# One PSUM tile for the four output banks, tiles visited two at a time, first products in sub-steps: a chunk attention with two FFNs on one core

## The chip, the cores and the metric

One core of one Trainium2 chip runs the kernel. The metric is the device time of one execution in microseconds; before the change it is 1147.26 us, the median of three runs from 1143.62 to 1149.77.

## The reference, cut to what matters

```python
for c in range(S // 32):                               # q, k, v: (4, 8, 768, 64)
    k_full = concat([mem_k, k[16 left, 32 own, 8 right]])   # the same for v
    a = softmax(q_c @ k_full.T / 8)
    out[c] = a @ v_full
x = out.transpose(0, 2, 1, 3).reshape(3072, 512)
g = s * max(x @ w_in, 0) ** 2 + b                      # first FFN, 512 -> 2048 -> 512
x = g @ w_out
h = x @ w_in2                                          # second FFN, same widths
y = (max(h, 0) + alpha * min(h, 0)) @ w_out2
```

## The kernel before

**Tiles and blocks.** The 3072 tokens are 24 attention tiles of 128 tokens, and four tiles make one of six blocks of 512. Each FFN walks over the blocks, and in a block over 16 slices f of the hidden width. One unit is one block with one f: a *first product* (`g1`, L597-608, 12 matmuls of 128x512 into a bank `ph`), the activation on ACT and DVE (L616-650), and a *second product* (`g2`, L651-666, three matmuls for each of four output parts d, into banks `po0` to `po3`, which add up over all f). The factor three is there because every fp32 number is split into a high and a low part in a shorter type, and high·high, high·low and low·high are summed. The weights come as 32-bit words from HBM and are split on chip by `convert` (L286-340) on DVE and ACT.

**Ends of a block.** After the last f of a block the four banks `po` are emptied: in the first FFN ACT writes the high part (L696), then DVE the low part (L700), and GpSimd's DMA queue stores both (`x1_out`, L703); in the second FFN d0 and d2 are copied by ACT (L712), d1 and d3 by DVE (L714), each into one of two buffers (`ao`), and stored. In the last block each copy is split into a half on ACT (L709) and a half on DVE (L710). Blocks 0 and 1 of the first FFN are run in two parts, the first SEG slices of both, and then the rest: at the end of a first part ACT copies the banks out (L676) and they are stored; at the end of the second part DVE adds them back (L688), and high and low are made from the sum. The next block's second products start in bank `po0` right after one more first product (12 matmuls), then follow d1, d2, d3.

**Attention.** A tile has scores (64 matmuls, L401), row maxima, exponentials, sums and normalisation on DVE and ACT, four transposes (*turns*, L466), values (64 matmuls, L488), and a high and a low part of the result on ACT and DVE (L507-514). Tiles 0 to 3 run alone at the start, in the `po` banks, which are free then: `ALONE` maps a tile to a pair of banks, and scores and values lie in two tiles of one bank each, so that DVE and ACT read each bank by an operation of its own (256 columns wide). For a later tile the matmuls are done in a *visit* in one double bank `pa`: scores of tile i and values of tile i-1 in a single step (`products`, L492), and then the turns of tile i by themselves (`turn_joint`, L500).

**Order.** Every step is planned with a duration, a rank, and the steps that it needs (classes `Plan`, `Pace`, `Step`, L70-220); the planner lists the steps by rank and by a model of when each can begin, and the program is emitted in that order (L903-908). The tables `FIRST_LOADS`, `TILE_RANKS`, `BY_HEAD`, `CONV_RANKS` and `STEPS` at the top steer it. The semaphore waits are put in when the program is built: an instruction waits for the last earlier user of a tile that it overwrites or reads. A tile is what one call of `psum.tile` returns.

Of the kernel before, what the change touches and what calls it, by code (L numbers as in the profile page):

```python
# [16 lines left out]
P = 128  # L17
# [10 lines left out]
BLK = 512  # L28
# [17 lines left out]
FIRST_LOADS = """q0 q1 w1i v0 q3 w0o q2 v2 w0i v1 w1o q4 v3 w2 w3 w4 v4 w6 q5 v7 q6 v5 q7 w5 w9 v6 w7 w8""".split()  # L46

TILE_RANKS = (-280, -85, -170, -175, -15, -240, -5, -260, -85)

BY_HEAD = (1, 2, 4, 5, 6)  # L50

CONV_RANKS = {1: 195, 2: 35, 3: 30, 4: 25, 5: 20, 6: 15, 9: -40, 10: -95, 11: -25, 12: -10, 13: 40, 14: -70}

STEPS = (28, 18, 18, 47, 43, 38)
# [28 lines left out]
class Pace:  # L83
# [3 lines left out]
    BLOCK, FIRST = 256, 184  # L87
# [14 lines left out]
    def run(self, t, step, fetch):  # L102

        done, total = 0, max(step.count, 1)
        while done < total:
            at = self.count + done
            block, into = divmod(at - self.FIRST, self.BLOCK)
            if block >= 0 and into == 0:
                t = max(t, self.due[block])
                self.due[block + 1] = t + fetch(t)  # L110
            n = min(total - done, self.BLOCK - into)
# [14 lines left out]
class Plan:  # L126
# [4 lines left out]
    RATE = 396e3  # L131
    LANES = 8
    FETCH = 2.7, 5.3
# [13 lines left out]
    def order(self):  # L147
# [17 lines left out]
        while len(done) < len(self.steps):  # L165
# [58 lines left out]
def tile_chunk_attention_two_ffn(ctx: ExitStack, tc: tile.TileContext, qt, kw, vw, win, wout, cst, out):  # L224
# [11 lines left out]
    xl = [const.tile([P, KD, BLK], F32R, name=f"xl{n}") for n in range(2)]  # L236
    x1d = [dram.tile([P, KD, 2, BLK], F32R, name=f"x1d{j}") for j in range(NB)]
# [27 lines left out]
    wts, raws, conv_done, load_done = {}, {}, {}, {}  # L265

# [19 lines left out]
    def convert(layer, f, mats, rank, after):  # L286
# [106 lines left out]
    def scores(i, banks=None):  # L393
        kd, qT = sets[set_of(i)][0], state[i]["q"]
        banks = banks or bank_pair(i, "sc")
        parts, both = banks if isinstance(banks, tuple) else (banks, None)
        for hp in range(HP):
            for c in range(NC4):
                for par in range(2):
                    r = slice(par * D, par * D + D)  # L400
                    nc.tensor.matmul(parts[par][c * CH:(c + 1) * CH, 0, hp, :],  # L401
                                     lhsT=qT[r, hp, c * CH:(c + 1) * CH], rhs=kd[r, hp, c * (CH + NM):c * (CH + NM) + NKEY],
                                     start=True, stop=True)
        state[i]["sc"] = pieces(parts, both, 0)

    def pieces(parts, both, which):

        if both is not None:
            return [(slice(0, 2), both[:, :, which])]
        return [(slice(par, par + 1), parts[par][:, which:which + 1]) for par in range(2)]  # L410
# [49 lines left out]
    def one_bank(i, name):  # L460
        return psum.tile([P, HP, P], F32, tag=f"po{2 * ALONE[i]}", name=name)
# [15 lines left out]
    def values(i, banks=None):  # L477
# [3 lines left out]
        parts, both = banks if isinstance(banks, tuple) else (banks, None)  # L481
        for half in range(HP // 2):
            for c in range(NC4):
                for odd in range(2):
                    for par in range(2):
                        r, hp = slice(par * D, par * D + D), 2 * half + odd
                        out = parts[par][odd * D:odd * D + D, 1].rearrange("p a n -> p (a n)")
                        nc.tensor.matmul(out[:, half * P + c * CH:half * P + (c + 1) * CH], lhsT=vd[r, c, hp, :],  # L488
                                         rhs=aT[r, hp, c * CH:(c + 1) * CH], start=True, stop=True)
        state[i]["px"] = [(pars, px.rearrange("p two (half a) n -> p two half (a n)", half=HP // 2)) for pars, px in pieces(parts, both, 1)]  # L490

    def products(prev, i):  # L492
# [26 lines left out]
    def softmax(i, r, sc):  # L519
        a = att[i]  # L520
        mx = plan.add("DVE", (0.8 if i % TB in (0, TB - 1) else 0.61) + (0.08 if i in ALONE else 0), r + STEPS[0], lambda: maxima(i), [sc])
# [6 lines left out]
        else:  # L528
            sh = plan.add("DVE", 0.61 + (0.08 if i in ALONE else 0), r + STEPS[0], lambda: shifted(i), [mx])
# [5 lines left out]
    def loads(i, r):  # L535
# [5 lines left out]
        a["lv"] = plan.add("SP", 0.45, first_load(f"v{i}") if early else r - 14, lambda: load_v(i), [left.get("v")], nbytes=1 << 19)  # L541
# [3 lines left out]
    def finish_tile(i, r, px):  # L545
        leaves[set_of(i)]["v"] = leaves[set_of(i)]["x"] = px
        more = 0.15 if i in ALONE else 0
# [433 lines left out]
```

## Time and profile before

| | |
|---|---|
| median of the runs | 1147.26 us |
| the profiled execution, its own time | 1147.76 us |
| its span in the trace | 1146.0 us |
| before and behind the span | 1.76 us |
| instructions in the span | 18300 |
| matmuls that the page lists on PE | 7848 |
| DMA traffic | 98.32 MB |

The span runs from the first to the last instruction of the trace. PE, DVE, ACT, POOL and SP are the five engines (TensorE, VectorE, ScalarE, GpSimd, SyncE), and PEld is the loading of weights into TensorE, which overlaps its matmuls. In a timeline a row gives the start, the duration, the engine, the source line, the operation and its tiles, and in brackets how long the engine was idle just before and what released it. The duration of a matmul covers its pipeline too, so that two that follow each other overlap; what a stream costs is read from the distance between starts.

### The profile page before, as it was taken

What the parts mean: (1) busy time and instruction counts of PE and PEld (TensorE: products, weight loads), DVE (VectorE), ACT (ScalarE), POOL (GpSimd) and SP (SyncE); (2) the same over time, 40 slices, a digit from 0 to 9 for tenths busy, and PEclk for the clock granted to TensorE, in tenths of its full rate; (3) what the DMA queues carried; (4) which work ended last, traced back from release to release, by engine and by line L of the source; (5) the groups of instructions that cost most, each with busy time, mean ns of one, the idle gap of its engine ahead of it and who ended that gap; (6) DMA issues with size and microseconds to landing.
All of it is one profiled execution on the core that took longest, in us unless ns stands there. A gap on an engine that the chain in (4) does not pass through costs nothing.

```text
span 1146.0 us, 18300 instructions
## 1 busy us (share of the span) xinstructions
PE 1117.8 (98%) x7848; PEld 926.0 (81%) x7848; DVE 607.9 (53%) x942; ACT 350.9 (31%) x615; POOL 28.8 (3%) x58
## 2 busy tenths in 40 slices
PE   4799999999999999999999999999999999999998
PEld 4788888888888888888887788888888888888886
DVE  6796945454544445434799844434433434344333
ACT  5675734332223223224565311111111111111111
POOL 0000000000000000000000000000000000000000
PEclk9899999999999999999999999999999999999999
DMA  9918013423113113004557102002002002000000
GB/s 345 351 38 302 10 66 110 146 82 125 51 42 138 42 42 134 1 1 170 198 184 255 76 1 101 10 1 94 17 1 92 19 1 89 23 1 4 34 1 37
DMA packets 46241, 98.32 MB, mean 86 GB/s; under 512 B 4944, under 2 KB 4944, under 8 KB 46160
## 3 DMA queue, kind: packets, MB, share of 16 engines
q1 hardware_dynamic: 40320, 77.22, 19.4%
q0 software_dynamic: 5696, 19.93, 4.6%
q8 instruction: 61, 1.00, 0.4%
q14 instruction: 20, 0.16, 0.0%
q10 hardware_dynamic: 144, 0.01, 0.0%
HBM read 76.16 MB, written 20.97 MB: 85 GB/s over the span
## 4 chain that ended last, share of the span: by engine, by line
PE 49%; issue 42%; DMA 3%; DVE 3%; POOL 1%; ACT 1%; SPq 0%; POOLq 0%; DVEq 0%; ACTq 0%
PE ph L605 24%; PE po L666 22%; PE po L664 2%; DMA raw<-in_win_dram 1%; POOL x1d L703 1%; DVE a L309 1%; DMA spill<-os 1%; DVE a L314 1%; DMA qT<-in_qt_dram 0%; PE sp L488 0%; DMA qa<-in_qt_dram 0%; DMA vd<-in_vw_dram 0%; DVE w L327 0%; DVE gl L649 0%; DMA x1d<-o 0%
## 5 line engine op out<-in xcount | busy, mean ns | idle before, releaser
L605 PE MATMUL ph<-xh,w 128*128 128x512 f32 (+1 forms) x1560 | 509.7, 389 | 1.6 <-issue 0.9
L605 PEld LDWEIGHTS ph<-xh,w 128*128 128x128 f32 x1560 | 293.7, 189 | 61.7 <-DVE g L636 1.1
L605 PE MATMUL ph<-xl,w 128*128 128x512 f32 (+1 forms) x780 | 302.0, 387 | 0.0
L644 ACT ACTIVATE gh<-g 128x512 fp32r<-128x512 f32 (+1 forms) x195 | 121.7, 624 | 465.8 <-DVE g L636 385.2
L664 PE MATMUL po<-gh,w 128*128 128x512 f32 (+1 forms) x792 | 257.9, 387 | 0.2 <-DVE o L688 0.2
L666 PE MATMUL po<-w,gh 128*128 128x512 f32 x768 | 251.6, 389 | 0.5 <-DVE o L700 0.5
L649 DVE TENSOR_TENSOR gl<-g,gh 128x512 fp32r<-128x512 f32 (+1 forms) x195 | 133.1, 683 | 101.7 <-ACT gh L644 100.2
L631 DVE TENSOR_SCALAR g<-ph,cst_sb 128x512 f32<-128x512 f32 x96 | 72.0, 750 | 213.2 <-PE ph L605 213.1
L664 PEld LDWEIGHTS po<-gh,w 128*128 128x128 f32 x792 | 148.7, 189 | 30.1 <-DVE o L688 0.7
L605 PEld LDWEIGHTS ph<-xl,w 128*128 128x128 f32 x780 | 147.6, 189 | 28.6
L666 PEld LDWEIGHTS po<-w,gh 128*128 128x128 f32 x768 | 144.1, 188 | 31.0 <-DVE o L700 1.2
L664 PE MATMUL po<-gl,w 128*128 128x512 f32 (+1 forms) x396 | 152.1, 384 | 0.0
L666 PE MATMUL po<-w,gl 128*128 128x512 f32 x384 | 149.4, 389 | 0.0
L616 ACT ACTIVATE g<-ph 128x512 f32<-128x512 f32 (+1 forms) x99 | 57.8, 584 | 137.7 <-PE ph L605 134.2
L664 PEld LDWEIGHTS po<-gl,w 128*128 128x128 f32 x396 | 75.0, 189 | 14.1
L623 DVE TENSOR_TENSOR g<-g 128x512 f32<-128x512 f32 x48 | 33.2, 692 | 97.0 <-ACT g L616 96.9
L666 PEld LDWEIGHTS po<-w,gl 128*128 128x128 f32 x384 | 72.1, 188 | 14.9
L627 DVE TENSOR_SCALAR g<-g,cst_sb 128x512 f32<-128x512 f32 (+1 forms) x99 | 52.6, 531 | 42.6 <-ACT g L621 41.3
L636 DVE SCALAR_TENSOR_TENSOR g<-ph,g 128x512 f32<-128x512 f32 x96 | 66.3, 690 | 2.9
L296 ACT ACTIVATE a<-raw 128x1024 f32<-128x1024 f32 (+1 forms) x36 | 37.6, 1045 | 22.6 <-DVE w L327 14.3
L321 ACT ACTIVATE w<-a 128x1024 fp32r<-128x1024 f32 (+1 forms) x36 | 34.8, 967 | 31.2 <-DVE a L314 30.1
L327 DVE TENSOR_TENSOR w<-a,w 128x1024 fp32r<-128x1024 f32 (+1 forms) x36 | 39.5, 1100 | 1.2 <-ACT w L321 1.2
(83 smaller groups left out, 517.6 us busy)
## 6 DMA issues: line engine op xcount, KB each, us to landing
raw<-in_win_dram SPq DMA_DIRECT2D x64, 256.0 KB, 4.7
raw<-in_wout_dram SPq DMA_DIRECT2D x64, 256.0 KB, 5.3
x1d<-o POOLq DMA_DIRECT2D x24, 512.0 KB, 3.4
vd<-in_vw_dram SPq DMA_DIRECT2D x40, 256.0 KB, 4.1
kd<-in_kw_dram SPq DMA_DIRECT2D x20, 368.0 KB, 5.0
xh<-x1d SPq DMA_DIRECT2D x6, 1024.0 KB, 5.6
xl<-x1d SPq DMA_DIRECT2D x6, 1024.0 KB, 7.6
qT<-in_qt_dram SPq DMA_DIRECT2D x20, 256.0 KB, 3.9
```

The source lines that it names most:

```text
L296: nc.scalar.activation(out=temp["a"], in_=words(1).bitcast(F32), func=ACTF.Abs)
L321: nc.scalar.activation(out=w[:, :, 0, :], in_=temp["a"], func=ACTF.Copy)
L327: nc.vector.tensor_sub(out=w[:, :, 1, :], in0=temp["a"], in1=w[:, :, 0, :].bitcast(F32))
L605: nc.tensor.matmul(p, lhsT=w[:, a, kk * P:(kk + 1) * P], rhs=x[:, kk, cols], start=(i == 0), stop=(i == 3 * KD - 1))
L616: nc.scalar.activation(out=new_g(u), in_=ph.pop(u), func=ACTF.Relu)
L627: nc.vector.tensor_scalar(out=g, in0=g, scalar1=cst_sb[:, 0:1], scalar2=cst_sb[:, 1:2], op0=ALU.mult, op1=ALU.add)
L631: nc.vector.tensor_scalar(out=new_g(u), in0=ph[u], scalar1=0.0, scalar2=cst_sb[:, 2 + f:3 + f], op0=ALU.min, op1=ALU.mult)
L636: nc.vector.scalar_tensor_tensor(out=g, in0=ph.pop(u), scalar=0.0, in1=g, op0=ALU.max, op1=ALU.add)
L644: nc.scalar.activation(out=gh, in_=gt[u], func=ACTF.Copy)
L649: nc.vector.tensor_sub(out=gl, in0=gt.pop(u), in1=gh.bitcast(F32))
L664: nc.tensor.matmul(po[d][:, cols], lhsT=w[:, a, ds_], rhs=g, start=start, stop=stop)
L666: nc.tensor.matmul(po[d], lhsT=g[:, ds_], rhs=w[:, a, :], start=start, stop=stop)
```

## The change

1. **One tile for the four output banks.** `po_all` is one PSUM tile of four banks, and `po[d]` a slice of it; the four tiles `po0` to `po3` are gone. Tiles 0 to 3 take two-bank slices of it too, and DVE and ACT read both banks by one operation 512 columns wide instead of two of 256.
2. **Tiles 8 to 23 two at a time** (`attention_of_two`): scores of two tiles in one visit, turns of two in the next, values of two in the third.
3. **First products in sub-steps**, for blocks 0 and 1 of the first FFN and f < 6: high·high first, then the four matmuls with the weight's low part and the four with x's low part, each a step of its own that needs only its own operands.
4. **The last block's copies** are no longer halved; all four are on ACT.
5. **The order:** SEG goes from 7 to 8, and the tables and some constants of the planner's model are new.

```diff
-SEG = 7
+SEG = 8
+APART = 6
...
+    po_all = psum.tile([P, KD, BLK], F32, name="po")
+    po = [po_all[:, d] for d in range(KD)]
...
         if i in ALONE:
-            return [psum.tile([P, 2, HP, D], F32, tag=f"po{2 * ALONE[i] + par}", name=name) for par in range(2)]
-        both = psum.tile([P, 2, 2, HP, D], F32, tag="pa", name=name)
+            both = po_all[:, 2 * ALONE[i]:2 * ALONE[i] + 2].rearrange("p b (two a n) -> p b two a n", two=2, a=HP)
+        else:
+            both = psum.tile([P, 2, 2, HP, D], F32, tag="pa", name=name)
...
     def one_bank(i, name):
-        return psum.tile([P, HP, P], F32, tag=f"po{2 * ALONE[i]}", name=name)
+        return po_all[:, 2 * ALONE[i]].rearrange("p (a n) -> p a n", a=HP)
...
+    def products_of_two(i, what, name):
+        banks = bank_pair(i, name)
+        for t in range(2):
+            what(i + t, banks, t)
+    def turn_two(i):
+        both = psum.tile([P, 2, HP, P], F32, tag="pa", name="turns")
+        for t in range(2):
+            turn(i + t, both[:, t])
...
+    def attention_of_two(i, r, r2, r3):
+        two = (i, i + 1)
+        for t in two:
+            loads(t, r, r2)
+        sc = plan.add("PE", 1.6, r, lambda: products_of_two(i, scores, "sc"),
+                      list(banks_free.get("pa", [])) + [att[t]["lq"] for t in two], count=256, dense=True)
...
+        pt = plan.add("PE", 0.65, r2, lambda: turn_two(i), [att[t]["e"] for t in two] + [id_], count=16)
...
+        px = plan.add("PE", 2.2, r3, lambda: products_of_two(i, values, "px"),
+                      [att[t]["aT"] for t in two] + [att[t]["lv"] for t in two], count=256, dense=True)
...
-    po = [None] * KD
...
     def g2(us, part, first, last):
         for d in part:
-            if first:
-                po[d] = psum.tile([P, BLK], F32, tag=f"po{d}", name=f"po{d}")
...
     def y_copy(j, d, scalar):
...
-        if scalar == 2:
-            half = BLK // 2
-            nc.scalar.activation(out=o[:, :half], in_=po[d][:, :half], func=ACTF.Copy)
-            nc.vector.tensor_copy(out=o[:, half:], in_=po[d][:, half:])
-        elif scalar:
+        if scalar:
             nc.scalar.activation(out=o, in_=po[d], func=ACTF.Copy)
...
+        if layer == 0 and j < 2 and f < APART:
+            his = [x_hi[j * TPB + t] for t in range(cols.start // P, cols.stop // P)]
+            s = plan.add("PE", 4 * mm, rank, lambda: g1(u, ((0, 0),), True, False), his + [conv_high[f], id_, in_turn[0]],
+                         takes=("ph", ("ph", u)), count=8)
+            rest = [(((1, 0),), [conv_done[layer, 0, f]]), (((0, 1),), xs)]
+            for n_, (kinds, needs) in enumerate(rest if f == 0 else rest[::-1]):
+                s = plan.add("PE", 4 * mm, rank, lambda kinds=kinds, n_=n_: g1(u, kinds, False, n_ == 1), [s, *needs], count=8)
```

**Place 1: TensorE at the end of the first block of the second FFN, before.** These are the second products of the block's last slice; `gh` and `gl` are the high and low part of the activation, `w` the weights, and what an instruction waits for stands behind it.

```order
L666 MATMUL po0_6252<-w_6477,gh_6710 128x512 [waits Activation_49]
L666 MATMUL po0_6252<-w_6477,gl_6711 128x512 [waits DVE_49]
L666 MATMUL po1_6301<-w_6477,gh_6710 128x512
L666 MATMUL po1_6301<-w_6477,gl_6711 128x512
L666 MATMUL po2_6305<-w_6477,gh_6710 128x512
L666 MATMUL po2_6305<-w_6477,gl_6711 128x512
L666 MATMUL po3_6327<-w_6477,gh_6710 128x512
L666 MATMUL po3_6327<-w_6477,gl_6711 128x512
```

The first two rows wait for the operands; what follows for d1, d2 and d3 waits for nothing. Next, the same place in the changed kernel: eight rows of TensorE, as far as the next block's d1 (`gh_6670`), then two of ScalarE and two of VectorE, the copies of d0, d2, d1 and d3; all four banks are the tile `po_78`.

```order
L691 MATMUL po_78<-w_6405,gh_6638 128x512 [waits Activation_49]
L691 MATMUL po_78<-w_6405,gl_6639 128x512 [waits DVE_49]
L691 MATMUL po_78<-w_6405,gh_6638 128x512 x2
L691 MATMUL po_78<-w_6405,gl_6639 128x512
...
L691 MATMUL po_78<-w_6405,gh_6638 128x512 [waits Activation_49]
...
L691 MATMUL po_78<-w_6405,gh_6638 128x512 [waits DVE_49]
...
L691 MATMUL po_78<-w_5556,gh_6670 128x512 [waits DVE_49]
...
L691 MATMUL po_78<-w_5556,gh_6670 128x512 [waits Activation_49]
L733 ACTIVATE y_6698<-po_78 128x512 [waits PE_49]
L733 ACTIVATE y_6735<-po_78 128x512 [waits DMASW1_49,DVE_49,PE_49]
L735 COPY y_6704<-po_78 128x512 [waits PE_49,Activation_49]
L735 COPY y_6728<-po_78 128x512 [waits DMASW0_49,PE_49]
```

The first matmul of d2 now waits for ACT's copy of d0, that of d3 for DVE's copy of d1, and in the next block d0 for DVE's copy of d3 and d1 for ACT's copy of d2. By the values of the semaphores the copy of d0 itself waits for the last matmul of d1, which stands ahead of it in the emitted order, the copy of d1 for the last of d2, that of d3 for the last of d3, and that of d2 for the last of the next block's d0.

**Place 2: the end of block 2 of the first FFN, changed kernel**, d0 to d3 on TensorE and the next unit's first product (`L634`), then two rows of ScalarE (high parts of d0 and d1) and two of VectorE (low parts).

```order
L689 MATMUL po_78<-gh_3635,w_1848 128x512 [waits Activation_49]
L689 MATMUL po_78<-gl_3636,w_1848 128x512 [waits DVE_49]
L689 MATMUL po_78<-gh_3635,w_1848 128x512 x2
...
L689 MATMUL po_78<-gh_3635,w_1848 128x512 [waits Activation_49]
...
L689 MATMUL po_78<-gh_3635,w_1848 128x512 [waits Activation_49]
...
L634 MATMUL ph_3784<-xh1_75,w_570 128x512
L721 ACTIVATE o_3769<-po_78 128x512 [waits DMASW6_49,PE_49]
L721 ACTIVATE o_3777<-po_78 128x512 [waits DMASW7_49,DVE_49]
L725 TENSOR_TENSOR o_3769<-po_78,o_3769 128x512 [waits DMASW6_49,PE_49,Activation_49]
L725 TENSOR_TENSOR o_3777<-po_78,o_3777 128x512 [waits DMASW7_49,PE_49,Activation_49]
```

Here d2 and d3 both wait for ACT. The high part of d1 waits for DVE's low part of d0, and that for the last matmul of d2. Before, the same two rows of ScalarE were these, with the rows behind them:

```order
L696 ACTIVATE o_3773<-po0_2898 128x512 [waits DMASW6_49,PE_49]
L696 ACTIVATE o_3778<-po1_2904 128x512 [waits DMASW7_49,PE_49]
L696 ACTIVATE o_3825<-po2_2959 128x512 [waits DMASW0_49,Activation_49]
L696 ACTIVATE o_3847<-po3_2966 128x512 [waits DMASW1_49,Activation_49]
L700 TENSOR_TENSOR o_3773<-po0_2898,o_3773 128x512 [waits DMASW6_49,Activation_49]
L700 TENSOR_TENSOR o_3778<-po1_2904,o_3778 128x512 [waits DMASW7_49,Activation_49]
```

None of the high parts waited for a low part then, and no second product of another bank for either.

**Place 3: TensorE's first visits, before and then changed.** `sc` and `pt` are a lone tile's scores and turns, `px` its values, `sp` the scores of tiles 4 and up.

```order
L401 MATMUL sc<-kd,qT 32x64 [waits DMAHW4_49,DMAHW3_49]
L466 MATMUL pt<-ident,e 128x128 [waits DVE_49,Activation_49,Pool_49]
L488 MATMUL px<-aT,vd 64x32 [waits DMAHW7_49,Activation_49]
L401 MATMUL sc<-kv,qa 32x64 [waits DMAHW6_49,DMAHW5_49,DVE_49]
L401 MATMUL sp<-kd,qT 32x64 [waits DMAHW7_49,DMAHW0_49]
L605 MATMUL ph<-xh_74,w 128x256 [waits Activation_49]
L605 MATMUL ph<-xl_76,w 128x256
```

```order
L409 MATMUL po<-kd,qT 32x64 [waits DMAHW4_49,DMAHW3_49,DVE_49]
L468 MATMUL po<-ident,e 128x128 [waits DVE_49,Activation_49,Pool_49]
L490 MATMUL po<-aT,vd 64x32 [waits DMAHW7_49,Activation_49]
L409 MATMUL po<-kv,qa 32x64 [waits DMAHW6_49,DMAHW5_49,Activation_49]
L634 MATMUL ph<-xh_74,w 128x256 [waits Activation_49]
L634 MATMUL ph<-xh_74,w 128x256 x3
L409 MATMUL po<-kv,qa 32x64 [waits DMAHW1_49,DMAHW2_49,DVE_49,Activation_49]
L409 MATMUL sp<-kd,qT 32x64 [waits DMAHW7_49,DMAHW0_49]
```

The second tile's scores now wait for DVE as well, because the first tile's scores are read from the same tile; the first first-product, here its four high·high matmuls, stands ahead of the last lone tile's scores and no longer behind the scores of tile 4 (`sp`).

More of the change, by code (lines that the diff above doesn't have):

```diff
@@ L109, in run @@
                 t = max(t, self.due[block])
+            if block >= 0 and into == self.AHEAD:
                 self.due[block + 1] = t + fetch(t)
-            n = min(total - done, self.BLOCK - into)
+            n = min(total - done, self.AHEAD - into if into < self.AHEAD else self.BLOCK - into)
             work = step.cost * n / total
@@ L340, in convert @@
             conv_done[layer, m, f] = lo
+        if layer == 0 and 0 in mats:
+            conv_high[f] = hi
     sets = {}
@@ L400, in scores @@
                     r = slice(par * D, par * D + D)
-                    nc.tensor.matmul(parts[par][c * CH:(c + 1) * CH, 0, hp, :],
+                    nc.tensor.matmul(parts[par][c * CH:(c + 1) * CH, at, hp, :],
                                      lhsT=qT[r, hp, c * CH:(c + 1) * CH], rhs=kd[r, hp, c * (CH + NM):c * (CH + NM) + NKEY],
                                      start=True, stop=True)
[L404 to L410, printed above, removed]
+        state[i]["sc"] = [(slice(0, 2), both[:, :, at])]
     def maxima(i):
@@ L475, in normal, with values @@
         nc.vector.tensor_tensor(out=e, in0=e, in1=state[i]["rs"].unsqueeze(3).to_broadcast([P, 2, HP, NKEY]), op=ALU.mult)
-    def values(i, banks=None):
+    def values(i, banks=None, at=1):
         vd, aT = sets[set_of(i)][1], state[i]["aT"]
         banks = banks or bank_pair(i, "px")
-        parts, both = banks if isinstance(banks, tuple) else (banks, None)
+        parts, both = banks
         for half in range(HP // 2):
@@ L528, in softmax @@
         else:
-            sh = plan.add("DVE", 0.61 + (0.08 if i in ALONE else 0), r + STEPS[0], lambda: shifted(i), [mx])
+            sh = plan.add("DVE", 0.61, r + STEPS[0], lambda: shifted(i), [mx])
             ex = plan.add("ACT", 0.53, r + STEPS[1], lambda: exps(i), [sh])
@@ L546, in finish_tile @@
         leaves[set_of(i)]["v"] = leaves[set_of(i)]["x"] = px
-        more = 0.15 if i in ALONE else 0
-        hi = plan.add("ACT", 0.49 + more, r + STEPS[5], lambda: x_high(i), [px] + list(x_users[i // TPB % 2]))
-        x_done[i] = plan.add("DVE", 0.61 + more, r + STEPS[5], lambda: x_low(i), [hi])
+        hi = x_hi[i] = plan.add("ACT", 0.49, r + STEPS[5], lambda: x_high(i), [px] + list(x_users[i // TPB % 2]))
+        x_done[i] = plan.add("DVE", 0.61, r + STEPS[5], lambda: x_low(i), [hi])
         return x_done[i]
@@ L781, in plan_finish @@
                 end = j == NB - 1
-                c = plan.add("ACT" if d % 2 == 0 or end else "DVE", 0.35 if end else 0.6, rank + 6,
-                             lambda d=d: y_copy(j, d, 2 if end else d % 2 == 0), [lasts[d]], takes=("ao", h))
+                scalar = d % 2 == 0 or end
+                c = plan.add("ACT" if scalar else "DVE", 0.6, rank + 6, lambda d=d, scalar=scalar: y_copy(j, d, scalar),
+                             [lasts[d]], takes=("ao", h))
                 plan.add("SP" if end else "PQ", 0.5, rank + 6, lambda d=d: y_out(j, d, nc.sync if end else nc.gpsimd),
```

74 lines of the change are left out of this document (41 added, 33 removed).

## The prediction

> **What bounds the kernel now.** The profile's page comes first: span, busy engines, granted clock.
>
> ```profile
> span 1146.0 us, 18300 instructions
> PE 1117.8 (98%) x7848; PEld 926.0 (81%) x7848; DVE 607.9 (53%) x942; ACT 350.9 (31%) x615; POOL 28.8 (3%) x58
> PEclk9899999999999999999999999999999999999999
> ```
>
> TensorE is busy for 98% of the span, every other computing engine far less, and its clock is granted nearly all the time. So an edit pays only if it removes TensorE work or one of its few gaps, and whatever makes TensorE wait is paid in full. Where the gaps are is seen in the busy times by stretch (columns: stretch, length, busy time and count of PE, PEld, DVE, ACT, POOL; then granted clock, DMA share, GB/s).
>
> ```profile
> 20.00:40.00 20.00, 14.56 (x488) 12.98 (x479) 19.49 (x44) 15.36 (x54) 0.00 (x0) 0.99 0.97 346
> 40.00:60.00 20.00, 16.75 (x259) 16.29 (x254) 13.44 (x25) 11.60 (x33) 0.00 (x0) 0.75 1.03 373
> 60.00:80.00 20.00, 20.00 (x226) 17.17 (x225) 19.86 (x30) 14.95 (x35) 0.00 (x0) 1.00 0.01 5
> 80.00:100.00 20.00, 19.29 (x147) 15.93 (x146) 19.66 (x28) 13.29 (x21) 0.68 (x1) 1.00 0.64 224
> 600.00:700.00 100.00, 98.79 (x434) 80.89 (x434) 72.86 (x95) 32.28 (x44) 2.13 (x4) 1.00 0.27 96
> 900.00:1000.00 100.00, 100.00 (x443) 82.81 (x442) 40.79 (x59) 13.21 (x21) 2.17 (x4) 1.00 0.09 32
> ```
>
> In 900 to 1000, deep in the second FFN, TensorE never pauses: 443 matmuls in 100 us, one each 0.2257 us. A block of that FFN is 384 matmuls or 87 us long, so one block end lies in it, and it shows no gap. In 20 to 60 it is idle for 8.7 us while DMA is at 0.97 to 1.03 of its engines and DVE is busy for 19.49 of the first 20 us; then DVE is full (19.86, 19.66) up to 100 us.
>
> The costliest groups of second products confirm that block ends are free: the last column is the idle time of TensorE before them, and who ended most of it.
>
> ```profile
> L664 PE MATMUL po<-gh,w 128*128 128x512 f32 (+1 forms) x792 | 257.9, 387 | 0.2 <-DVE o L688 0.2
> L666 PE MATMUL po<-w,gh 128*128 128x512 f32 x768 | 251.6, 389 | 0.5 <-DVE o L700 0.5
> ```
>
> In all, 0.7 us was lost to waiting for an eviction (L688, L700).
>
> **The change part by part. First the single PSUM tile.** In the built program a second product into bank d2 now waits for the copy of d0, and that copy for the last matmul of d1 (place 1). TensorE therefore stands still from the last matmul of d1 until the copy is over. What that handshake costs is read in the timeline at the first block end of the second FFN, on either engine:
>
> ```profile
> 709.26 0.61 PE L666 MATMUL po<-w,gh 128*128 128x512 f32 x2
> 709.69 0.60 ACT L712 ACTIVATE y<-po 128x512 f32<-128x512 f32 x1 [3.90 <-PE po L666]
> 709.94 0.61 PE L666 MATMUL po<-w,gh 128*128 128x512 f32 x2
> 710.41 0.68 DVE L714 COPY y<-po 128x512 f32<-128x512 f32 x1
> ```
>
> The first row holds the last matmul of d0, at its start, and the first of d1; ACT's copy begins 0.43 us behind and takes 0.60. On DVE it is 710.41 − 709.94 = 0.47 and 0.68. How TensorE gets going again is seen at a wait for DVE and one for ACT:
>
> ```profile
> 628.75 0.68 DVE L636 SCALAR_TENSOR_TENSOR g<-ph,g 128x512 f32<-128x512 f32 x1
> 629.48 0.50 PE L605 MATMUL ph<-xh,w 128*128 128x512 f32 x1 [0.72 <-DVE g L636]
> 629.82 0.40 PE L605 MATMUL ph<-xl,w 128*128 128x512 f32 x1
> 14.87 0.60 ACT L471 ACTIVATE aT<-pt 128x512 f32<-128x512 f32 x1
> 15.52 1.93 PE L488 MATMUL px<-aT,vd 64*64 64x32 f32 x64 [0.69 <-ACT aT L471]
> ```
>
> DVE ends at 629.43 and TensorE starts 0.05 later; ACT ends at 15.47 and it starts 0.05 later. The next matmul comes 0.34 behind the first, against the pitch of 0.2257: 0.11 more, and I add 0.05 for the pitches after it. The pitch itself would have passed anyway. One wait for ACT: 0.43 + 0.60 + 0.05 + 0.16 − 0.23 = **1.0 us**; one for DVE: 0.47 + 0.68 + 0.05 + 0.16 − 0.23 = **1.1 us**. Nothing covers them: no other TensorE work stands between the matmuls. Their bounds: 0.75 (the wait of 0.72 shown at 629.48, as good as the lower end) and 1.3, if the copy is behind one third of another DVE operation of 0.68.
>
> *Second FFN, five block ends:* d2 waits for ACT's copy of d0 (1.0), d3 for DVE's copy of d1 (1.1), and the next block's d1 for ACT's copy of d2, which waits for that block's d0 (1.0). The wait of the next d0 for the copy of d3 is hidden by the 12 matmuls of a first product (12 × 0.2257 = 2.7 us against 1.2). 5 × 3.1 = **15.5 us**.
>
> *First FFN:* the same handshake, with evictions of these durations:
>
> ```profile
> L696 ACT ACTIVATE o<-po 128x512 fp32r<-128x512 f32 x16 | 9.4, 596 | 9.0 <-DMA x1d<-o 7.8 <-DVE w L327 1.1
> L700 DVE TENSOR_TENSOR o<-po,o 128x512 fp32r<-128x512 f32 x16 | 10.9, 688 | 4.7 <-ACT o L696 4.4
> L688 DVE TENSOR_TENSOR o<-po,o 128x512 f32<-128x512 f32 x8 | 5.5, 688 | 1.0 <-DMA o<-spill 1.0
> L676 ACT ACTIVATE os<-po 128x512 f32<-128x512 f32 x8 | 4.5, 590 | 8.3 <-DMA spill<-os 6.9 <-DVE w L327 1.4
> ```
>
> 596 and 590 ns on ACT, 688 on DVE: the same prices. Ends of the first parts of blocks 0 and 1: one uncovered wait each, for ACT (2.0); of their second parts: one and two for DVE (1.1 + 2.2). Ends of blocks 2 and 3 (place 2): d2 waits for ACT's high part of d0 (1.0); d3 for a chain, since the high part of d1 waits for the low part of d0, and that for the last matmul of d2: 0.47 + 0.69 + 0.60 and two handovers of 0.05, with 0.16 of restart, less 0.23 of pitch, 1.8; and a like chain of two pairs for the next block's d2 ends about 0.4 behind the two first products that cover it: 3.2 each, 6.4. Block 4: 1.0, 1.1 and 0.4, so 2.5. From the first FFN to the second 24 matmuls mostly cover the chain; I take 1.0. Together 2.0 + 3.3 + 6.4 + 2.5 + 1.0 = **15.2 us**.
>
> *End of the kernel:* two handshakes (d2 for d0, d3 for d1) at 1.0 for ACT. Then two full copies come behind the last matmul, of d2 and d3, 2 × 0.60 = 1.20, where two halves did:
>
> ```profile
> 1137.41 0.38 ACT L709 ACTIVATE y<-po 128x256 f32<-128x256 f32 x1 [1.85 <-PE po L666]
> 1137.83 0.42 DVE L710 COPY y<-po 128x256 f32<-128x256 f32 x1 [1.54 <-ACT y L709]
> ```
>
> From 1137.41 to 1138.25 is 0.84. So 2.0 + 0.4 = **2.4 us**.
>
> **Tiles two at a time.** A visit of before, between second products:
>
> ```profile
> 165.03 0.39 PE L605 MATMUL ph<-xh,w 128*128 128x512 f32 x1
> 165.25 0.60 PE L466 MATMUL turns<-ident,e 128*128 128x128 f32 x4
> 165.61 0.48 PE L664 MATMUL po<-gh,w 128*128 128x512 f32 x1
> 166.85 0.40 PE L664 MATMUL po<-gh,w 128*128 128x512 f32 x1
> 167.18 0.86 PE L401 MATMUL sp<-kd,qT 64*32 64x64 f32 x64
> 167.97 1.14 PE L488 MATMUL sp<-aT,vd 64*64 64x32 f32 x64
> 169.03 0.50 PE L664 MATMUL po<-gh,w 128*128 128x512 f32 x1
> ```
>
> Scores take 0.79, values 1.06, and entering and leaving add 0.33 at 167.18 and 0.11 at the pitch behind 169.03 (0.34), less 0.23: 2.06. Turns cost 0.36 and 0.09 more of restart: 0.45. Two tiles cost 2 × (2.06 + 0.45) = 5.02. Paired, two scores 1.58 with entry 0.21, two values 2.12 with 0.21 (4.1 at most), less the overlap of a mixed visit that isn't there any more, say 3.85, and eight turns at four times 0.09 more with one entry, 0.88: 4.7. Eight pairs × 0.3 = **−2.5 us**; bounds −4 (every second entry free) and +1 (each entry of the longer visits 0.4 dearer than those of before).
>
> **Startup: sub-steps, two-bank views, order.** Before:
>
> ```profile
> 25.29 0.92 PE L401 MATMUL sp<-kd,qT 64*32 64x64 f32 x44 [2.00 <-issue]
> 27.03 0.58 PE L605 MATMUL ph<-xh,w 128*128 128x256 f32 x1
> 43.78 0.85 PE L488 MATMUL sp<-aT,vd 64*64 64x32 f32 x19 [3.25 <-issue]
> 44.56 0.58 PE L664 MATMUL po<-gh,w 128*128 128x256 f32 x1
> ```
>
> The first product begins at 27.03, the first second product at 44.56, and gaps of 2.00 and 3.25 with no releaser stand between. The sub-steps let TensorE start before the low parts are there: it gets about 2 us earlier to its first product (no `sp` visit ahead, place 3). But what the second products need is made by DVE, busy 19.49 of 20 us, and loaded at 346 to 373 GB/s; neither gets less by these edits, but for the wide operations that save four or so fixed parts. And the lone tiles are now chained through one tile: the second's scores wait for DVE to have read the first's. I take **−1 us**, bounds −6 (both gaps, 5.25, and a little) and +5 (a lone tile's chain later by four operations of 0.6 and the turns between). SEG 8 adds no work: the same units in another order.
>
> **The sum:** 15.5 + 15.2 + 2.4 − 2.5 − 1 = 29.6, say 30. The profiled execution took 1147.76 (1146.0 of span and 1.76 around it), 0.5 above the median of 1147.26. 1147.76 + 29.6 = **1177.4 us**.
>
> **The rivals.**
>
> *A: the waits cost nothing.* If the evictions are done before TensorE reaches the matmul, because the planner put other work between, or the waits pass, 15.5 + 15.2 + 2.0 go and −2.5 − 1 + 0.4 stay: 1144.7, not slower; at the ends −4 and −6 it is 1138. It decides if more than 1.0 to 1.1 us of other matmuls, five, stand between the copy and the matmul that waits. For it: before, DVE reads d1 at 710.41 while TensorE writes d2 (710.62 follows 709.94 at the usual pitch), and nothing is lost, so the chip has no need of the waits. Against it: the rows of places 1 and 2, where nothing stands between. 7%, of which 2 faster.
>
> By a rule of the Trainium skill the waits could be spared: "PSUM — Partial Sum Buffer", section "PSUM bank collisions raise a hardware error", says to guard PSUM by bank (and quadrant), and these copies and matmuls are in different banks. The trace of before agrees, as 0.7 us of waits at all block ends shows; by it rival A's 1144.7 would be the time of a program that guards by bank. The built program guards by tile, so I keep the sum.
>
> *B: the clock falls too.* If three stops of 1 us in 5 us count as idleness, each of the 13 ends (five in the second FFN, eight in the first) is followed by some 4 us at half speed, as TensorE had from 44.56 on in the stretch with a granted clock of 0.75: 2 us × 13 = 26 more, 1203. Against it: behind the wait of 0.72 at 629.48 the pitch is 0.34, then normal, and the granted clock of 600 to 700 is 1.00. 4%.
>
> The Trainium skill, "TensorE: Matmul & The Clock Gate", section "A second HAM failure mode: psum-queue depth-cycling", tells of a kernel whose clock swings when it cycles through banks with small pauses. By that rule 1203 would come out; no row here shows pauses so close together in a warm stretch.
>
> *C: the start gets worse.* If the chained lone tiles delay DVE's conversions, which have no slack up to 100 us, it is +8 in place of −1: 1186. For it: DVE at 19.49 and 19.86 of 20. Against it: the first product stands earlier. 7%.
>
> **How the numbers follow.** Main case 82%, A 7, B 4, C 7. With 27 or so handshakes of the two kinds, an error of 0.25 in each is ±7; the bounds of the visits and the start add −6.5 and +9.5 if all come together, which they hardly do: 1163 to 1190 in the main case. That takes in C and leaves out A and B; 0.89 of the cases lie in it by the list, about 0.8 with the tails of the main case. A difference of 0.5% (5.7 us) is about what a measurement can tell from none. Faster 0.02, same 0.05, slower 0.93.
>
> **What would show it.** In the profile after: the groups of second products have some 25 to 30 us of idle time before them, ended by the copies on ACT and DVE, in place of 0.7; the stretch 900 to 1000 holds about 429 matmuls with one block end in it or 416 with two, not 443, at a clock of 1.00; timelines at block ends show three gaps of 0.7 to 1.0 us. Right in direction and wrong in size if the gaps are there but shorter. Wrong altogether if those groups show no idle time (A), if the clock falls below 0.95 behind the ends (B), or if the first second product starts later than 46 us (C).

## The result, and the profile after

The changed kernel takes 1182.5 us, the median of four runs (1180.0 to 1184.6), beside 1147.6 for the kernel before: a ratio of 1.032, 95% interval 1.029 to 1.035. It is slower by 34.9 us; forecast were 1177.4, between 1163 and 1190. The profiled execution took 1180.0, with a span of 1178.2, 32.2 longer than that of before. Two executions further down (3960 us of e6_single, 2266 us of e8_halves) were in a slow state and are left out of the times there.

The page of after: span, busy engines, and the two groups of second products (idle time before them in the last column).

```profile
span 1178.2 us, 18295 instructions
PE 1125.7 (96%) x7848; PEld 923.0 (78%) x7848; DVE 604.6 (51%) x926; ACT 352.9 (30%) x626; POOL 28.7 (2%) x58
L689 PE MATMUL po<-gh,w 128*128 128x512 f32 (+1 forms) x792 | 261.5, 388 | 12.7 <-ACT o L721 5.0
L691 PE MATMUL po<-w,gh 128*128 128x512 f32 x768 | 256.3, 392 | 14.8 <-DVE y L735 8.4
```

The number of matmuls is the same, TensorE's share of the span fell from 98 to 96%, and the two groups that had waited 0.7 us now wait 27.5. What is named as the end of the wait is a copy out of a bank. The timeline of after at the first block end of the second FFN shows one handshake after another:

```profile
722.08 0.39 PE L691 MATMUL po<-w,gh 128*128 128x512 f32 x1
722.51 0.60 ACT L733 ACTIVATE y<-po 128x512 f32<-128x512 f32 x1 [4.57 <-PE po L691]
723.15 0.50 PE L691 MATMUL po<-w,gh 128*128 128x512 f32 x1 [0.69 <-ACT y L733]
723.49 0.40 PE L691 MATMUL po<-w,gl 128*128 128x512 f32 x1
723.73 0.39 PE L691 MATMUL po<-w,gh 128*128 128x512 f32 x1
724.22 0.69 DVE L735 COPY y<-po 128x512 f32<-128x512 f32 x1 [1.60 <-PE po L691]
724.97 0.50 PE L691 MATMUL po<-w,gh 128*128 128x512 f32 x1 [0.85 <-DVE y L735]
```

From the last matmul of d1 (722.08) to the first of d2 (723.15) it is 1.07 us instead of 0.2257; the next pitch is 0.34, and over the next three 0.12 more than usual is lost. So a wait for ACT costs 0.85 + 0.12, and one for DVE 724.97 − 723.73 − 0.23 = 1.01 and 0.12. Forecast were 1.0 and 1.1.

The third stop of each end comes behind the first product of the next unit, and it isn't the one that was forecast:

```profile
726.08 0.60 ACT L733 ACTIVATE y<-po 128x512 f32<-128x512 f32 x1 [2.46 <-PE po L691]
731.23 0.39 PE L691 MATMUL po<-w,gh 128*128 128x512 f32 x1
731.72 0.69 DVE L735 COPY y<-po 128x512 f32<-128x512 f32 x1 [0.66 <-PE po L691]
732.46 0.50 PE L691 MATMUL po<-w,gh 128*128 128x512 f32 x1 [0.84 <-DVE y L735]
```

ACT copies d0 and d2, DVE d1 and d3. ACT's copy of d2 (726.08) waited for the last matmul of d3 and is over long before the next block's second products begin at 730.10. DVE's copy of d3 waited for the sixth of those, the last of d1 (731.23), and the first of d2 for that copy: 732.46 − 731.23 − 0.23 = 1.00, and 0.12. The rows listed for place 1 have these two copies in the other order (d3's first, d2's behind the next block's d0); in the program that ran, the late copy is the one on DVE.

The busy times of after by stretch (columns as in the prediction) show the start and the deep part:

```profile
20.00:40.00 20.00, 13.70 (x357) 12.09 (x358) 15.44 (x32) 13.46 (x53) 0.00 (x0) 1.00 1.01 368
40.00:60.00 20.00, 18.97 (x306) 17.24 (x305) 18.52 (x34) 16.96 (x46) 0.00 (x0) 1.00 0.85 299
900.00:1000.00 100.00, 96.11 (x419) 77.94 (x418) 38.78 (x55) 13.04 (x22) 3.78 (x7) 1.00 0.10 37
```

In 900 to 1000 stand 419 matmuls in place of 443; two block ends, at 905 and 995, lie in it, for which about 416 were forecast. At the start TensorE is idle 7.3 us from 20 to 60, before 8.7; but DVE, full before from 20 to 40 (19.49), now has 4.6 us of idle time there.

To place the 32.2 us I took each distance between two matmuls' starts in both traces, less the distance that its form has in a gapless stretch (0.2257 for 128x512), and added up by stretch. Of after: from 100 to 600 us 22.4 are lost (before 8.6), from 600 to 700 3.0 (2.4), from 700 to 1110 19.6 (1.7), behind that 2.2 (0.1), and ahead of 100 us 27.0 (29.5). That is +13.9, +0.6, +17.9, +2.1 and −2.5, and 0.2 more from the last matmul's start to the end: 32.2.

### The profile page after: what moved, and what is told of

Read it like the earlier page. It is cut to its first block, busy times and chain, and to the rows that moved or that the text cites. A ratio compares the mean times of both kernels' runs of the same rounds, so it can differ in the third digit from the quotient of the medians.

```text
span 1178.2 us, 18295 instructions
## 1 busy us (share of the span) xinstructions
PE 1125.7 (96%) x7848; PEld 923.0 (78%) x7848; DVE 604.6 (51%) x926; ACT 352.9 (30%) x626; POOL 28.7 (2%) x58
## 4 chain that ended last, share of the span: by engine, by line
PE 52%; issue 40%; DMA 4%; ACT 1%; POOL 1%; DVE 1%; SPq 1%; ACTq 0%; POOLq 0%; DVEq 0%
PE ph L634 25%; PE po L691 23%; PE po L689 4%; DMA raw<-in_win_dram 1%; POOL x1d L728 1%; DMA x1d<-o 1%; DMA spill<-os 1%; DVE y L735 1%; DMA raw<-in_wout_dram 1%; DMA kv<-in_kw_dram 1%; DMA kv<-in_vw_dram 0%; ACT y L733 0%; PE sp L490 0%; SPq L285 0%; PE turns L468 0%
## 5 line engine op out<-in xcount | busy, mean ns | idle before, releaser
L634 PE MATMUL ph<-xh,w 128*128 128x512 f32 (+1 forms) x1560 | 503.8, 389 | 3.1 <-ACT xh L522 2.8
L634 PEld LDWEIGHTS ph<-xh,w 128*128 128x128 f32 x1560 | 292.8, 190 | 63.7 <-ACT xh L522 3.0
L634 PE MATMUL ph<-xl,w 128*128 128x512 f32 (+1 forms) x780 | 295.7, 389 | 0.0
L689 PE MATMUL po<-gh,w 128*128 128x512 f32 (+1 forms) x792 | 261.5, 388 | 12.7 <-ACT o L721 5.0
L691 PE MATMUL po<-w,gh 128*128 128x512 f32 x768 | 256.3, 392 | 14.8 <-DVE y L735 8.4
L634 PEld LDWEIGHTS ph<-xl,w 128*128 128x128 f32 x780 | 146.4, 190 | 29.5
L691 PEld LDWEIGHTS po<-w,gl 128*128 128x128 f32 x384 | 72.1, 188 | 14.2
```

Source lines behind the costliest of these rows:

```text
L634: nc.tensor.matmul(ph[u], lhsT=w[:, a, kk * P:(kk + 1) * P], rhs=x[:, kk, cols], start=first and i == 0, stop=last and i == len(each) - 1)
L689: nc.tensor.matmul(po[d][:, cols], lhsT=w[:, a, ds_], rhs=g, start=start, stop=stop)
L691: nc.tensor.matmul(po[d], lhsT=g[:, ds_], rhs=w[:, a, :], start=start, stop=stop)
```

## The experiments

Three theories. *T*: the one tile does it, since waits are put in by tile. *O*: the new order starves the second products, and the tile only decides what is named. *C*: the lone tiles' chain costs at the start as well. The first four kernels ran on one chip beside the kernel before (1147.6).

**e1_four: four tiles again, all else as in the change.**

```diff
-    po_all = psum.tile([P, KD, BLK], F32, name="po")
-    po = [po_all[:, d] for d in range(KD)]
+    po = [psum.tile([P, BLK], F32, name=f"po{d}") for d in range(KD)]
...
+            return [po[2 * ALONE[i] + par].rearrange("p (two a n) -> p two a n", two=2, a=HP) for par in range(2)], None
...
+        return po[2 * ALONE[i]].rearrange("p (a n) -> p a n", a=HP)
```

> The changed kernel with four PSUM tiles of one bank for the output again, and the lone tiles' two banks read by two operations; all else stays. Theory T (the one tile makes the builder put waits between banks): the 30 stops of TensorE at block ends, which sum to 33.4 us in the profile of after, go, and 1182.5 - 33.4 = 1149 us, between 1146 and 1151; no stop over 0.25 us at the ends of blocks 0 to 4 of the first FFN and all blocks of the second. Rival O (the new order, with its visits of two and sub-steps, starves the second products, and the tile only decides which instruction is named): the stops stay for the most part, 1165 us or more.

Measured: 1135.0 us (1134.3 to 1135.3), ratio to before 0.9885, interval 0.987 to 0.990. 47.5 us under the changed kernel, and 12.6 under the kernel before. Its two groups, and its stretches at the start:

```profile
L694 PE MATMUL po<-w,gh 128*128 128x512 f32 x768 | 251.5, 389 | 0.0
L692 PE MATMUL po<-gh,w 128*128 128x512 f32 x744 | 247.7, 393 | 0.6 <-ACT os L704 0.6
20.00:40.00 20.00, 16.27 (x356) 14.21 (x352) 19.52 (x45) 18.66 (x73) 0.00 (x0) 1.00 1.05 382
40.00:60.00 20.00, 20.00 (x309) 18.09 (x309) 19.59 (x31) 15.57 (x40) 0.00 (x0) 1.00 0.77 281
```

The stops are gone, O falls, and T stands, but 14 us more went than T said. The same sum over matmul starts shows where: ahead of 100 us it loses 20.7, after 27.0. DVE is full again from 20 to 40, and TensorE idle for 3.7 us from 20 to 60.

**e2_pairs: two tiles of two banks.**

```diff
-    po_all = psum.tile([P, KD, BLK], F32, name="po")
-    po = [po_all[:, d] for d in range(KD)]
+    po_two = [psum.tile([P, 2, BLK], F32, name=f"po{n}") for n in range(2)]
+    po = [po_two[d // 2][:, d % 2] for d in range(KD)]
```

> The changed kernel with two PSUM tiles of two banks (d0 and d1, d2 and d3), so that the lone tiles keep their wide operations. By the order as built every second product that waits for a copy has 12 matmuls (2.7 us) or more between it and what the copy waits for. Theory T: as with four tiles, 1146 to 1151 us. Rival S (any sharing of a tile by two banks costs its handshakes): half of the 33.4 us stays, some 1166 us. Rival O: 1165 us or more.

Measured: 1141.6 us, ratio 0.9943 (0.993 to 0.996). All the lead at the start is there (19.1 lost ahead of 80 us, in e1_four 19.4), so sharing by two does not harm it. But the span is 5.6 us longer than that of e1_four: my count of cover (12 matmuls are 2.7 us) was too simple where a copy waits for more than a matmul. At the end of block 0's first part:

```profile
95.50 0.39 PE L689 MATMUL po<-gh,w 128*128 128x512 f32 x1
97.37 0.60 ACT L701 ACTIVATE os<-po 128x512 f32<-128x512 f32 x1 [1.23 <-DMA spill<-os]
98.02 0.50 PE L689 MATMUL po<-gh,w 128*128 128x512 f32 x1 [2.13 <-ACT os L701]
```

The copy waits for its buffer, which a store holds, and hands that wait on to TensorE: 2.3 us are lost there, in e1_four 0.75 at the same place. Another stop of 1.1 stands at 344 us, each of the five ends of the second FFN loses 0.4, and the end of the kernel 0.7.

**e3_one: the kernel before with the one tile alone.**

```diff
+    po_all = psum.tile([P, KD, BLK], F32, name="po")
+    po = [po_all[:, d] for d in range(KD)]
...
-            return [psum.tile([P, 2, HP, D], F32, tag=f"po{2 * ALONE[i] + par}", name=name) for par in range(2)]
+            return [po_all[:, 2 * ALONE[i] + par].rearrange("p (two a n) -> p two a n", two=2, a=HP) for par in range(2)]
...
-                po[d] = psum.tile([P, BLK], F32, tag=f"po{d}", name=f"po{d}")
```

> The kernel before with one PSUM tile of four banks for the output and for the lone tiles, which are still read by two operations; nothing else is changed. As built, 10 stops without cover in the second FFN (d2 for ACT, d3 for DVE at each end), 9 in the first and 2 at the end of the kernel, each 0.85 to 1.0 plus 0.12 of restart: 21 x 1.05 = 22. Theory T: 1147.6 + 22 = 1170 us, within 1166 to 1174. Rival C (the lone tiles, chained through one tile, delay the start): 8 us more at the start, 1178 us. Rival O: 1147 to 1152 us, the waits are hidden in this order.

Measured: 1187.9 us (1183.8 to 1191.3), ratio 1.0345 (1.032 to 1.037): the one tile alone costs 40.3 us in the order of before. The size was missed because the count was: the trace shows 30 stops of 0.85 to 1.6 us behind 100 us, where 21 were counted, three and not two at each end of the second FFN. That trace is of the fastest run, 36.0 us above the profiled run of before; the slowest of the four has the lowest mean granted clock, 0.991 against 0.997, so a part of the 40.3 is the clock, of which more below. C adds little here: ahead of 100 us 28.9 are lost, before 29.5, of which some 2.4 are a fall of the clock that e3_one doesn't have.

**e4_late: the changed kernel, with the second FFN's copies emitted behind d3.**

```diff
-                             [lasts[d]], takes=("ao", h))
+                             [lasts[d if end else KD - 1]], takes=("ao", h))
```

> The changed kernel, one tile of four banks, but in the second FFN (all blocks but the last) each copy is planned behind the last second product of d3, and so emitted behind it. Every matmul that waits for a copy then has the 12 matmuls of a first product ahead of it. Theory T: the 15 stops of the second FFN go (16.0 us with their restarts), those of the first FFN stay: 1182.5 - 16 = 1166.5 us, within 1163 to 1170. Rival B2 (the chip itself cannot read one bank while TensorE writes another of the same tile without loss): copies now run beside first products only, the same 1166. Rival O: within 3 us of 1182.5.

Measured: 1166.0 us (1162.3 to 1168.2), ratio to before 1.0153 (1.013 to 1.018), 16.5 less than the changed kernel. Its groups: the second FFN waits 3.2 where it waited 14.8, the first as ever.

```profile
L691 PE MATMUL po<-w,gh 128*128 128x512 f32 x768 | 252.0, 389 | 3.2 <-DVE o L725 1.8 <-ACT y L733 1.4
L689 PE MATMUL po<-gh,w 128*128 128x512 f32 x744 | 251.5, 396 | 11.9 <-ACT o L721 5.0 <-ACT os L701 2.9 <-DVE o L713 2.3
```

The same tile, the same copies: emitted behind the last matmul of the block, they have a first product for cover. From 700 to 1110 us the matmul starts now lose 1.7, as much as before the change. This run alone doesn't part T from B2, since no copy runs beside another bank's second product here; e1_four does, where the copies run beside them again and the second FFN waits 0.0.

**What the rest of the change is worth.** e1_four is faster than before by 12.6 us. The next four take parts out of it, or put one back. They ran in a second round, without e1_four itself; the kernel before took 1146.6 there (22 runs), and e8_halves, which differs from e1_four in the last copies alone, 1135.2.

A part of that lead is the clock. Before, TensorE runs at a granted clock of 0.50 for 10.24 us around its gap of 3.25:

```profile
39.59:49.83 10.24, 6.99 (x80) 6.80 (x74) 4.69 (x10) 3.35 (x11) 0.00 (x0) 0.50 1.01 361
```

From 44.56 to 49.84 it starts 24 matmuls of 128x256, 0.22 us each instead of 0.12, which is 2.4 us. e1_four has no such stretch. Of the 22 runs of before, the two at a mean clock of 1.000 took 1141.8 and 1142.2 us, those at 0.995 or less 1146.6 to 1148.8; so against e1_four some 7 us are left where the clock holds.

*e5_whole*, no sub-steps:

```diff
-APART = 6
+APART = 0
```

> e1_four without the sub-steps: every first product is one step of 12 matmuls again. The traces put 9.3 us of e1_four's lead over the kernel before (at 50 us into the span: 22.8 us behind a gapless TensorE against 32.1) at the start. Theory U (the sub-steps bring it, since TensorE needs no low parts to begin): most of it goes, 1142 to 1145 us. Theory V (the order of loads and conversions brings it): within 2 us of e1_four, 1134 to 1137.

Measured: 1141.1 us, 6.1 more than e1_four. The timeline of TensorE names the low halves, of the weight and of x:

```profile
34.18 0.39 PE L637 MATMUL ph<-xh,w 128*128 128x256 f32 x1 [1.40 <-DVE w L331]
39.43 0.39 PE L692 MATMUL po<-gh,w 128*128 128x256 f32 x1 [1.59 <-DVE xl L529]
```

U is right in kind, but the time is 0.9 under its range: half of the lead is theirs.

*e6_single*, visits as before:

```diff
-            attention_of_two(i, *visits[i])
+            attention(i - 1 if i > 2 * TPB else None, i if i < NTILE else None, visits[i], visits[i] + 20)
```

> e1_four with tiles 8 to 23 visited one at a time as before (scores of one with values of the one ahead, turns apart). From 100 to 600 us e1_four loses 4.9 us against a gapless TensorE, the kernel before 8.5. Theory W (that is the pairing): +3.6, 1138.6 us, within 1137.5 to 1140, and the start unchanged. The prediction's own term was 2.5: 1137.5. Rival X (the pairing is worth nothing, the difference is other edits): within 1 us of 1135.

Measured: 1138.2 us, 3.2 more than e1_four: W, and X falls.

*e7_tables*, the five tables of before and SEG 7:

```diff
-SEG = 8
+SEG = 7
...
-STEPS = (59, 89, 62, 132, 93, 79)
+STEPS = (28, 18, 18, 47, 43, 38)
```

> e1_four with the tables of before (order of the first loads, ranks of tiles and conversions, steps, tiles by head, SEG 7), everything else as in e1_four. Theory V (the order of loads and conversions brings the lead at the start): most of 9.3 us goes, 1141 to 1145 us. Theory U (the sub-steps bring it): 1135 to 1138 us.

Measured: 1140.2 us, 5.2 more than e1_four. V has its part too, if a little under its range; its trace has a granted clock of 0.50 again, from 34.28 on for 6.83 us, so that part of the 5.2 is the clock. 6.1, 5.2 and 3.2 add up to 14.5, some 2 us more than the 12.6; overlap or noise between the two rounds, these runs don't tell.

*e8_halves*, the last copies halved:

```diff
+        if scalar == 2:
+            half = BLK // 2
+            nc.scalar.activation(out=o[:, :half], in_=po[d][:, :half], func=ACTF.Copy)
+            nc.vector.tensor_copy(out=o[:, half:], in_=po[d][:, half:])
```

> e1_four with the last block's copies split in halves on ACT and DVE again. By the prediction's term the two full copies behind the last matmul cost 1.20 against 0.84: 0.4 us less than e1_four, 1134.6 us; on the chip the span's end lies 0.3 to 0.5 us nearer to the last matmul. Rival: the split has no effect that can be measured, since the last store's landing sets the end either way: 1135.0 within 0.5.

Measured: 1135.2 us (1134.8 to 1135.7), no effect that can be measured. With four tiles the copy of d2 runs beside the matmuls of d3, so that one full copy stands at the end, not two: the last copy ends 1.08 us behind the start of the last matmul (1129.60 − 1128.52 in the timeline of e1_four), with halves 1.54 (1129.67 − 1128.13), since ACT's half waits for a buffer that a store still holds and DVE's half for ACT's.

**Does the clock fall?** In the trace of after there are two places where TensorE runs at half its pace, 0.425 us a matmul. The stretches (the last three columns are the granted clock, the DMA share and GB/s):

```profile
251.20:254.60 3.40, 3.40 (x9) 2.63 (x8) 1.54 (x3) 0.00 (x0) 1.06 (x2) 0.50 0.47 182
725.80:728.90 3.10, 3.10 (x9) 2.38 (x8) 0.00 (x0) 0.60 (x1) 0.54 (x1) 0.50 0.45 169
```

Eight matmuls at 0.20 more are 1.6 to 1.7 us each time. The unaltered kernels were profiled again, the changed one twice and the one before once, on another chip than the experiments above.

> The changed kernel once more, unaltered. In the trace of after TensorE runs at half its pitch (0.425 us a matmul, granted clock 0.50) for 3.4 us behind the stops at 249 and 724 us, 1.7 us lost each time, and at none of the other 11 ends. Theory G (the stops let the clock fall when they meet its window, by chance): the profiled execution has another number of such stretches, at other ends, and its time is 1176.6 + 1.7 per stretch, within 1. Rival H (the clock falls at fixed places): the same two places, the same 1180.0 within 0.7.

> As e9_again, a third profiled execution of the changed kernel. Theory G: 1176.6 us + 1.7 per stretch at half pitch, within 1, at ends that differ from those of the others. Rival H: stretches at 251 and 726 us, 1180.0 within 0.7.

> The kernel before once more, unaltered; its runs spread from 1143 to 1150 where those of e1_four lie within 1.1 us. In its trace the granted clock is 0.51 from 40 to 50 us, behind gaps of 1.73 and 3.25. Theory G: no stretch at half pitch behind 100 us, and what differs from 1147.76 us lies ahead of 100 us. Rival H: the same 1147.8 within 0.7, with the same cold stretch.

Measured: e9_again 1181.7 us, with two stretches (253 and 728 us); e10_again 1182.3 us with four, in these windows:

```profile
106.60:109.90 3.30, 3.30 (x9) 2.55 (x8) 3.23 (x5) 0.42 (x1) 0.00 (x0) 0.50 1.05 397
451.30:454.70 3.40, 3.40 (x9) 2.63 (x8) 0.69 (x1) 0.00 (x0) 0.53 (x1) 0.50 0.46 177
816.70:819.80 3.10, 3.10 (x9) 2.38 (x8) 0.00 (x0) 0.60 (x1) 0.71 (x2) 0.50 0.36 137
908.80:912.10 3.30, 3.30 (x9) 2.62 (x8) 0.00 (x0) 0.60 (x1) 0.54 (x1) 0.50 0.42 159
```

e11_before took 1148.5 us, with none behind 100 us and the long one at the start once more (40.51 to 50.75), so it parts the two theories no further. e1_four has none. The two ends of e9_again are those of after, as H has it, though not its time; the four of e10_again are others, and there H falls. What holds of G is the price, 1.7 us each, and that the stretches stand behind stops, 8 times at 39 ends. As a formula for the time it misses e10_again by 1.1 (1176.6 + 6.8 = 1183.4), just outside the 1 that it allowed, and e9_again by 1.7, which its trace has at the start (28.9 lost ahead of 100 us, not 27.0).

Which ends fall can be read from the traces, since the granted clock is recorded with them. Each of these stretches is 3.413 us long, and within one execution their starts lie whole multiples of that apart: 251.22 and 725.67 in after, 474.45 = 139 × 3.4133; in e10_again 106.58, 451.33, 816.56 and 908.72, which are 101, 107 and 27 such steps apart. So each trace can be cut into steps of 3.413 us. Around the first of after:

```profile
247.81:251.22 3.41, 1.84 (x8) 1.16 (x8) 2.26 (x4) 1.37 (x3) 0.00 (x0) 1.00 0.00 0
251.22:254.63 3.41, 3.41 (x10) 2.64 (x9) 1.52 (x3) 0.00 (x0) 1.06 (x2) 0.50 0.48 185
254.63:258.04 3.41, 3.41 (x16) 2.82 (x15) 1.24 (x2) 0.88 (x2) 0.00 (x0) 1.00 0.74 214
```

In the step ahead of the fall TensorE loses 2.03 us between matmul starts; its row has 1.57 of idle time, since the busy time counts the pipeline's end and the slow pitch behind a stop. Behind 100 us the three executions of the changed kernel have 8 falls, e4_late three (253.25, 454.63, 550.21) and e3_one two (451.48, 1089.77). All 13 follow a step in which 1.96 to 2.53 us were lost, and no other step lost more than 1.95. The clock thus falls for one step when enough of the stops lie within the step ahead of it, and since the steps lie elsewhere against the program in each execution, the same end falls in one and not in the next. That is the order of 13 cases, found after the runs and not forecast; how sharp the border is, and whether it holds for other work, isn't shown.

## Why the prediction was right

| term | forecast, us | measured, us | shown by |
|---|---|---|---|
| second FFN, five ends | 15.5 | 16.2, and 1.7 of half clock | matmul starts, e4_late (16.5) |
| first FFN, ends of blocks 0 to 4 | 14.2 | 15.4, and 1.7 of half clock | matmul starts (13.9), with the 3.2 of pairing added |
| first to second FFN | 1.0 | 0.6 | matmul starts |
| end of the kernel | 2.4 | 2.3 | matmul starts and the last copy |
| pairing | −2.5 | −3.2 | e6_single |
| start | −1 | −2.5 | matmul starts |
| sum | 29.6 | 32.2 | spans |

The sum is that of the two profiled executions. The medians lie 34.9 apart, because the other three runs of the changed kernel took 2.1 to 4.6 us more than the profiled one. That the sum came so near is in part luck: the 3.4 us of half clock that it left out are offset by a start and a pairing that came out 2.2 us better than forecast.

**The mechanism** stands as it was put: copies and matmuls of different banks are ordered by one tile, and nothing covers the gap. What the prediction did not count on is the clock. That it is the tile is shown by e1_four, where four tiles take 47.5 us away, and by e3_one, where one tile adds 40.3. That the emitted order decides is shown by e4_late.

**The price of a handshake**, 1.0 and 1.1, is 0.97 and 1.13 in the trace. In the second FFN one of the three was named wrongly: the prediction has the next block's d1 wait for ACT's copy of d2, at 1.0, and calls the copy of d3 hidden; in the trace the copy of d2 is hidden, and the next block's d2 waits for DVE's copy of d3, at 1.13. Five times 0.97 + 1.13 + 1.13 is 16.2, the measured sum. The chain at the end of block 2 is as long as forecast, too: 351.36 − 349.50 − 0.23 = 1.63 and 0.12 of restart, against 1.8.

```profile
349.50 0.40 PE L689 MATMUL po<-gh,w 128*128 128x512 f32 x1
349.99 0.69 DVE L725 TENSOR_TENSOR o<-po,o 128x512 fp32r<-128x512 f32 x1 [1.36 <-ACT xh L522]
350.71 0.60 ACT L721 ACTIVATE o<-po 128x512 fp32r<-128x512 f32 x1 [1.36 <-DVE o L725]
351.36 0.50 PE L689 MATMUL po<-gh,w 128*128 128x512 f32 x1 [1.47 <-ACT o L721]
```

**First FFN, mis-sized by 1.2.** "One uncovered wait each, for ACT (2.0)" at the ends of the first parts of blocks 0 and 1 measured 2.35 and 0.85, with 0.12 each. The first is the stop that e2_pairs shows too: in the timeline of after the copy (105.01 us) had waited 1.24 us for a buffer that a store still held. A copy that hands its wait on to TensorE passes on its own waits with it.

**Rival B was not wrong as a mechanism**, only its extent. It was given 4% as a fall of the clock behind each of 13 ends, 2 us each; the runs show 1.7 us behind two to four of the 13. The argument against it (no fall behind the single wait of 0.72 at 629.48) was about one short stop; these stretches stand behind two stops close together, or once, in e10_again, a single one that loses 2.55 us. The Trainium skill, "TensorE: Matmul & The Clock Gate", "A second HAM failure mode: psum-queue depth-cycling", describes such swings of the clock behind short pauses at PSUM; the windows above, at 0.50 for 3.4 us, agree with it.

**The start came out right by two errors.** The prediction had −1, from "neither gets less by these edits" on one side and the chain on the other; measured is −2.5, made of −8.8 (e1_four against before, 20.7 against 29.5) and +6.3 (after against e1_four, 27.0 against 20.7). The bound of −6 was too near: the sub-steps and the tables are worth 6.1 and 5.2 where four tiles are kept, and of the 8.8 some 2.4 are the stretch at a clock of 0.50 that before has and e1_four hasn't. DVE was taken to be full, so that no order could win time; but from 40 to 60 us it was busy for 13.44 of 20 before, as a row quoted in the prediction showed, and that row was read for TensorE alone. In e1_four it is 19.59. Rival C's mechanism is real as well, with 6.3 us here and, the clock set aside, some 2 in e3_one; it is the chain and not the reads of two banks by one operation, since e2_pairs keeps these and has the start of e1_four. In the trace of after it looks like this: tile 1's exponentials (L454) on ACT wait for tile 0's turns on TensorE, since both are in the one tile, and tile 0's values wait for the exponentials. These rows account for 1.7 us of the 6.3; the rest I have not traced.

```profile
12.14 1.09 PE L468 MATMUL po<-ident,e 128*128 128x128 f32 x4 [3.31 <-ACT e L454]
13.27 0.31 ACT L454 ACTIVATE e<-po,nm 128x64 f32<-128x64 f32 x1 [1.23 <-PE po L468]
14.44 0.61 ACT L473 ACTIVATE aT<-po 128x512 f32<-128x512 f32 x1
15.69 1.93 PE L490 MATMUL po<-aT,vd 64*64 64x32 f32 x64 [2.46 <-ACT e L454]
```

In e1_four those turns begin at 12.19, the same time, and the values at 13.97:

```profile
12.19 1.09 PE L471 MATMUL po<-ident,e 128*128 128x128 f32 x4 [3.75 <-DVE e L480]
13.97 1.92 PE L493 MATMUL po<-aT,vd 64*64 64x32 f32 x63 [0.69 <-ACT aT L476]
```

**Rival A** is what e1_four is, a program whose waits go by bank. It takes 1135.0 and not the 1144.7 worked out, mostly by the same error at the start: 8.8 and not the 1 that was left there. The rule of the Trainium skill weighed beside it, "PSUM — Partial Sum Buffer", "PSUM bank collisions raise a hardware error", to guard by bank, is borne out: with it TensorE's second products wait 0.6 us in all (e1_four), and the output needs no wait between banks.

## What to carry to other kernels

Where the builder puts in waits by tile, a tile is a unit of synchronisation: banks that are filled and emptied in turn belong in tiles of their own, even if a common view would save an operation. Before such an edit, count the places where a copy is emitted between two groups of matmuls, and the matmuls that could cover it; a stop costs the copy's latency, the copy, and whatever the copy itself waits for. And a change that is slower as a whole can hold parts that are faster: here all of it but the one tile gives 1135.0 us, 1.1% under the kernel before.

## What was not expected of the hardware

Stops that lose 1.96 to 2.53 us within one step of 3.413 us, two stops of 0.85 to 1.6 us or once a single one, were followed by a granted clock of 0.50 for the whole next step, at 8 of 39 block ends of the changed kernel. It costs 1.7 us each time, 3 to 7 us an execution, and which ends it strikes changes by chance with where the steps lie. e1_four, without such stops, varies by 1.0 us over four runs (1134.3 to 1135.3), the changed kernel by 4.6 and e3_one by 7.5. A kernel without stops at its block ends isn't safe by that alone: before varies by 7.1 over 22 runs (1141.8 to 1148.8), in the main the faster the higher its mean clock (1.000 to 0.994), and in both of its traces the fall is at the start, behind gaps.
